# A linear-attention and MLP kernel: the first five tiles written out piece by piece, in order of arrival

## The chip, the cores and the metric

One core of a Trainium2 chip. The metric is the device time of one execution in microseconds, as a median over runs; every comparison is made with runs of the kernel before on the same chip, in the fast state. Ratios are computed as the mean time of one kernel's fast runs over that of the other's of the same rounds, so they are not quite the ratio of the quoted medians. A profile's span is 1.7 to 1.9 us shorter than the timed execution it belongs to.

## The reference

```python
# r, k, v: (4, 8, 768, 48); per step t, with a (48 x 48) state per head
cur = outer(u * k_t, v_t);  y_t = r_t @ (state + cur);  state = w[:, None] * state + outer(k_t, v_t)
# then on x = y as (4, 768, 384):
xn = (x - mean) / sqrt(var + 1e-6) * g_ln
out = x + relu(xn @ w_ch1) @ w_ch2          # w_ch1: 384 x 1536, w_ch2: 1536 x 384
```

## The kernel before

The sequence is cut into chunks of 128 steps, 24 "tiles" in all. A tile goes through: load r, k, v; scale r (GpSimd) and k (VectorE) by powers of w; transposes on TensorE and a copy on ScalarE (`trs`); scores on TensorE, a mask on VectorE (`A`), the state (`Z`); values (`y`), x, statistics; centering on ScalarE (`xn`), the pow for the deviation on GpSimd (`rs`); transposes (`xT`); "ups" (x by w1, ReLU on ScalarE) and "downs" (by w2), then `ot` and the store. Ups of two tiles run together as a group (`GT = 2`, 256 columns). All five engines run their instructions in the order in which the program lists them. `fill(n)` puts in up to n queued ups or downs, which keeps TensorE busy while attention waits for other engines.

```python
scale(0); transposes(0)
for s in range(NT):
    if s + 1 < NT: scale(s + 1)            # r on GpSimd, k on VectorE, one tile ahead
    scores(s)
    if s >= 1: center(s - 1)               # xn on ScalarE, rs on GpSimd (last of a pair)
    if s == 1: scale_w1(0)
    if s + 4 < NT: load(s + 4)
    if s == 1: nc.gpsimd.dma_start(out=w2_sb[:], in_=w2_src)
    fill(2)
    if s + 1 < NT: transposes(s + 1)       # before the values of this tile
    fill(2)
    if s >= 1: ln_transposes(s - 1)        # queues the ups of a finished pair
    values(s)
    if s == 1: scale_w1(1); scale_w1(2)
    fill(2)
# ... (cut: end of the program)
```

Loads before the loop: w_c, chunk 0 (k on ScalarE's queue), chunk 1, w1, chunk 2, chunk 3.

## Time and profile before

| | before |
|---|---|
| time, median | 174.94 us of 3 runs (175.16 of 4 with the run beside the change) |
| span of the profile | 173.4 us |
| TensorE busy | 146.9 us, 85% |
| VectorE, ScalarE, GpSimd busy | 66%, 55%, 43% |
| first down matmul, last matmul ends | 39.3, 169.8 us |

The page's busy slices and the timelines are in the prediction. Two more views are wanted later. First, busy time by stretch of 10 us: for each engine (TensorE, its weight loads, VectorE, ScalarE, GpSimd) the busy time and the number of instructions, then the granted clock (the share of TensorE's full clock that the trace records), the DMA share and GB/s.

```profile
20.00:30.00 10.00, 4.04 (x44) 2.81 (x43) 7.84 (x16) 5.02 (x8) 9.08 (x12) 1.00 1.33 179
30.00:40.00 10.00, 10.00 (x113) 7.84 (x113) 5.65 (x13) 5.90 (x12) 2.66 (x5) 1.00 1.13 194
40.00:50.00 10.00, 9.24 (x107) 6.91 (x106) 8.19 (x17) 6.09 (x11) 5.54 (x8) 1.00 0.76 143
```

TensorE is 40% busy from 20 to 30 us and nearly full from there on. Second, of the groups by line, the two large matmul groups; the columns behind the last bar are TensorE's idle time just before them and what ended it.

```profile
L374 PE MATMUL hp<-xT,w_sb 128*128 128x256 bf16 x432 | 58.0, 276 | 2.7 <-ACT xT L359 2.7
L396 PE MATMUL o<-w_sb,hT 128*128 128x384 bf16 x288 | 56.3, 326 | 0.9 <-DVE ot L405 0.8
```

In the steady state, nearly all that is left of TensorE's idle time is ups that wait for ScalarE's xT and one down that waits for the output tile.

### The profile page before, as it was taken

To read this page: it belongs to the slowest core of one execution; us is meant where nothing else is said; L and a number is where in the kernel's file an instruction comes from. 1 tells how busy PE (TensorE), PEld (TensorE's weight loads), DVE (VectorE), ACT (ScalarE), POOL (GpSimd) and SP (SyncE) were. 2 spreads that over 40 slices of the span, in tenths; PEclk is the share of its full clock that TensorE was granted. 3 is DMA by queue.
4 is the path that set the end of the run, shared out by engine and by line. 5 is a ranking of instruction groups with operands and counts; after the bars stand their busy time and mean duration, and the time that the engine had idled before them with its cause. 6 is when DMAs were issued, how large, how long until landed. Compare 5 with 4: busy or idle time off the path is not lost.

```text
span 173.4 us, 4126 instructions
## 1 busy us (share of the span) xinstructions
PE 146.9 (85%) x1646; PEld 110.4 (64%) x1646; DVE 113.9 (66%) x236; ACT 94.6 (55%) x173; POOL 74.7 (43%) x119
## 2 busy tenths in 40 slices
PE   0327453998999999999999999999999999999981
PEld 0215242695786877777768767777778687686640
DVE  4407959549788688678767976786768667840111
ACT  0313273385585774675666647656666577565410
POOL 2292699057426553374255335642752453120000
PEclk9999999999999999999999999999999999999999
DMA  5999999999954755874686568546954011101121
GB/s 98 163 351 316 186 181 177 200 190 150 199 114 95 169 114 104 167 155 89 140 165 147 110 110 183 131 105 135 181 112 119 0 49 45 33 18 45 45 93 46
DMA packets 82739, 22.69 MB, mean 131 GB/s; under 512 B 76960, under 2 KB 81568, under 8 KB 82720
## 3 DMA queue, kind: packets, MB, share of 16 engines
q1 hardware_dynamic: 78896, 21.04, 59.1%
q0 software_dynamic: 1552, 1.18, 4.6%
q10 hardware_dynamic: 2272, 0.20, 1.1%
q8 instruction: 13, 0.21, 0.6%
q14 instruction: 6, 0.05, 0.1%
HBM read 18.88 MB, written 4.72 MB: 136 GB/s over the span
## 4 chain that ended last, share of the span: by engine, by line
PE 76%; DVE 10%; ACT 8%; issue 2%; DMA 1%; POOL 1%; DVEq 0%; ACTq 0%
PE hp L374 27%; PE o L396 25%; PE tr L214 7%; PE at L229 4%; ACT xT L359 3%; ACT trs L216 3%; PE tr L358 3%; PE s L240 2%; PE s L260 2%; PE y L312 2%; DMA w_c<-in_w_dram 1%; PE s L251 1%; PE y L300 1%; DVE ot L405 1%; DVE stats L326 1%
## 5 line engine op out<-in xcount | busy, mean ns | idle before, releaser
L374 PE MATMUL hp<-xT,w_sb 128*128 128x256 bf16 x432 | 58.0, 276 | 2.7 <-ACT xT L359 2.7
L396 PE MATMUL o<-w_sb,hT 128*128 128x384 bf16 x288 | 56.3, 326 | 0.9 <-DVE ot L405 0.8
L381 ACT ACTIVATE hT<-hp 128x512 bf16<-128x512 f32 x72 | 42.9, 598 | 22.6 <-PE hp L374 22.1
L279 POOL TENSOR_TENSOR Vb<-vf,cc 128x384 f32<-128x384 f32 x24 | 20.2, 841 | 66.2 <-ACT cc L277 66.2
L374 PEld LDWEIGHTS <-w_sb 128*128 128x128 bf16 x432 | 40.3, 99 | 9.0 <-issue 3.8
L396 PEld LDWEIGHTS <-hT 128*128 128x128 bf16 x288 | 27.6, 98 | 13.6 <-issue 1.4
L270 DVE TENSOR_TENSOR A<-at,mask 128x512 bf16<-128x512 f32 x48 | 30.7, 682 | 1.3 <-PE at L229 1.3
L216 ACT COPY trs<-tr 128x1024 bf16<-128x1024 bf16 x24 | 24.2, 1009 | 13.2 <-PE tr L214 13.2
L218 DVE TENSOR_TENSOR q<-trs 128x512 bf16<-128x512 bf16 x24 | 12.3, 512 | 25.2 <-ACT trs L216 25.1
L205 POOL TENSOR_TENSOR sc<-rk,F 128x384 bf16<-128x384 f32 x24 | 23.9, 997 | 2.4 <-DMA rk<-in_r_dram 2.4
L405 DVE SCALAR_TENSOR_TENSOR ot<-o,rs,x 128x384 f32<-128x384 f32 x24 | 14.6, 609 | 14.6 <-PE o L396 14.6
L214 PE MATMUL tr<-ident,sc 128*128 128x128 bf16 x192 | 16.7, 234 | 7.4 <-POOL sc L205 5.7
L214 PEld LDWEIGHTS <-sc 128*128 128x128 bf16 x192 | 13.6, 105 | 10.2 <-POOL sc L205 6.5
L322 DVE TENSOR_TENSOR x<-y,Vb 128x384 f32<-128x384 f32 x24 | 13.4, 556 | 9.1 <-PE y L312 9.0
L337 ACT ACTIVATE xn<-x,mv 128x384 bf16<-128x384 f32 x24 | 14.8, 617 | 0.7 <-DVE mv L330 0.7
L277 ACT COPY cc<-s 128x8 f32<-128x8 f32 x24 | 4.0, 166 | 20.2 <-PE s L260 17.8
L359 ACT COPY xT<-tr 128x384 bf16<-128x384 bf16 x24 | 11.5, 480 | 5.5 <-PE tr L358 5.5
L204 DVE TENSOR_TENSOR sc<-rk,F 128x384 bf16<-128x384 f32 x24 | 14.4, 599 | 0.0
L207 POOL CAST vv<-vf 128x384 bf16<-128x384 f32 x24 | 14.3, 595 | 0.0
L326 DVE BATCH_NORM_STATS2 stats<-x 128x6 f32<-128x384 f32 x24 | 13.5, 561 | 0.8
L358 PE MATMUL tr<-ident,xn 128*128 128x128 bf16 x72 | 8.2, 225 | 4.3 <-ACT trs L216 4.3
L229 PE MATMUL at<-trs 48*128 48x128 bf16 x192 | 10.4, 233 | 1.7 <-ACT trs L216 1.7
(49 smaller groups left out, 119.1 us busy)
## 6 DMA issues: line engine op xcount, KB each, us to landing
rk<-in_r_dram SPq DMA_DIRECT2D x24, 192.0 KB, 4.1
vf<-in_v_dram SPq DMA_DIRECT2D x24, 192.0 KB, 4.2
out_dram<-ot SPq DMA_DIRECT2D x24, 192.0 KB, 2.0
rk<-in_k_dram SPq DMA_DIRECT2D x23, 192.0 KB, 3.4
w_f<-in_moe_w_ch_dram SPq DMA_DIRECT2D x3, 768.0 KB, 6.1
w_sb<-in_moe_w_ch_dram POOLq DMA_DIRECT2D x1, 1152.0 KB, 12.5
rk<-in_k_dram ACTq DMA_DIRECT2D x1, 192.0 KB, 3.6
w_p<-in_w_dram ACTq DMA_DIRECT2D x2, 0.8 KB, 4.3
```

Of the source, the lines that this page charges most:

```text
L205: nc.gpsimd.tensor_tensor(out=sc[:, 0, :, :D], in0=rk_t[i][:, 0], in1=F2[:, 0], op=ALU.mult)
L214: nc.tensor.transpose(out=tp[:, j, :], in_=sc[:, j, :], identity=ident[:])
L216: nc.scalar.copy(out=tr[:], in_=tp[:].rearrange("p (a q) t -> p a q t", a=2))
L229: nc.tensor.matmul(out=at[:, par, p, :], lhsT=tr[p0 : p0 + D, 1, p, :], rhs=tr[p0 : p0 + D, 0, p, :], start=True, stop=True,)
L270: nc.vector.tensor_tensor(out=A[:, par], in0=at[:, par], in1=mask[:].unsqueeze(1).to_broadcast([P, HP, P]), op=ALU.mult,)
L279: nc.gpsimd.tensor_tensor(out=Vb[:], in0=vf_t[i][:], in1=cc[:].unsqueeze(2).to_broadcast([P, H, D]), op=ALU.mult)
L326: nc.vector.bn_stats(out=stats[:], in_=x[:])
L359: nc.scalar.copy(out=xT_t[g][:, :, j * P : (j + 1) * P], in_=tp[:, :CK, :])
L374: nc.tensor.matmul(out=hp[:, f, :], lhsT=w1_sb[:, n, kc, fb * P : (fb + 1) * P], rhs=xT_t[g][:, kc, :], start=(kc == 0), stop=(kc == CK - 1),)
L381: nc.scalar.activation(out=hT_t[g][:, 2 * m : 2 * m + 2, :], in_=hp[:], func=ACT.Relu)
L396: nc.tensor.matmul(out=o[:, :C], lhsT=hT_t[g][:, fk, j * P : (j + 1) * P], rhs=w2_sb[:, fk, :], start=(fk == 0), stop=(fk == FK - 1),)
L405: nc.vector.scalar_tensor_tensor(out=ot[:], in0=o[:, :C], scalar=rs_t[g][:, j : j + 1], in1=x_t[i][:], op0=ALU.mult, op1=ALU.add,)
```

## The change

It wants to fill the lead-in. Chunks 0 to 2 are loaded before w1, and each tile's work is listed when its data should have arrived. The first four tiles are groups of one, so that ups can start with the first tile. w2 is issued behind tile 3's casts. The steady state changes too: ups two slots after their transposes, output tiles that alternate between `o` and the `hp` buffers, scales two tiles ahead.

```diff
-    load(0, nc.scalar) ... load(1); w1; load(2); load(3)
+    for i in range(3): load(i)
+    w1
+    for i in range(3, 5): load(i)
...
-                ups.append((clock[0] + 1, g, m))
+                ups.append((clock[0] + 2, g, m))
+    group_len = [1] * 4 + [GT] * ((NT - 4) // GT)
...
-            o_t[i] = ps.tile([P, 512], FP32, name="o")
+            alt = not ups and i % 2
+            o_t[i] = ps_h.tile([P, 512], FP32, name="hp") if alt else ps.tile([P, 512], FP32, name="o")
...
+    scores(2)
+    center(1)
+    scale_w1(1)
+    fill(1)
+    ln_transposes(1)
+    values(2)
+    scale_w1(2)
+    fill(1)
+    center(2)
+    drain_ups()
+    for s in (3, 4):
+        scale_r(s)
+        scale_k(s)
+        transposes(s)
+        if s == 3:
+            nc.gpsimd.dma_start(out=w2_sb[:], in_=w2_src)
+        load(s + 2)
+        ln_transposes(s - 1)
+        scores(s)
+        drain_ups()
+        values(s)
+        center(s)
+    ln_transposes(4)
+    drain_ups()
+    w2_ready[0] = True
+    scale_r(5)
+    scale_k(5)
+    fill(6)
+    transposes(5)
+    scale_r(6)
+    load(7)
+    fill(3)
+    for s in range(5, NT):
+        ...  (the loop of before, scales two tiles ahead)
```

(Cut: the F factors in two PSUM tiles, tile 0's copy split between ScalarE and VectorE, w1's scaling without VectorE, seven hT buffers, a down that may follow a down when no up can run, tiles 0 to 2 up to scores(2).)

More of the change, by code (lines that the diff above doesn't have):

```diff
@@ L64, with load @@
     rk_t, vf_t, v_t = {}, {}, {}
-    def load(i, k_eng=None):
+    def load(i):
         b, c = divmod(i, NCH)
@@ L70, in load @@
         vf = ld.tile([P, H, D], FP32, name="vf")
-        (k_eng or nc.sync).dma_start(out=rk[:, 1], in_=k[b, :, s0 : s0 + L, :].rearrange("h t d -> t h d"))
-        nc.sync.dma_start(out=rk[:, 0], in_=r[b, :, s0 : s0 + L, :].rearrange("h t d -> t h d"))
-        nc.sync.dma_start(out=vf[:], in_=v[b, :, s0 : s0 + L, :].rearrange("h t d -> t h d"))
+        for dst, src in ((rk[:, 0], r), (rk[:, 1], k), (vf[:], v)):
+            nc.sync.dma_start(out=dst, in_=src[b, :, s0 : s0 + L, :].rearrange("h t d -> t h d"))
         rk_t[i], vf_t[i] = rk, vf
@@ L77 @@
     nc.sync.dma_start(out=w_c[:], in_=bass.AP(tensor=w.tensor, offset=w.offset, ap=[[1, P], [P, CK]]))
-    load(0, nc.scalar)
     w_p = const.tile([P, HP], FP32, name="w_p")
@@ L90 @@
     nc.scalar.dma_start(out=g_sb[:], in_=moe_g_ln.rearrange("(kc p) -> p kc", p=P))
-    load(1)
     NW = 3
@@ L95 @@
     w1_src = moe_w_ch1.rearrange("(kc p) (n f) -> p n kc f", p=P, n=NW)
-    for n in range(NW):
-        nc.sync.dma_start(out=w1_f[:, n], in_=w1_src[:, n])
     w1_sb = const.tile([P, NW, CK, FW], BF16, name="w1_sb")
@@ L100 @@
     w2_src = moe_w_ch2.rearrange("(fk p) c -> p fk c", p=P)
-    load(2)
-    load(3)
+    for i in range(3):
+        load(i)
+    for n in range(NW):
+        nc.sync.dma_start(out=w1_f[:, n], in_=w1_src[:, n])
+    for i in range(3, 5):
+        load(i)
     ident_f = const.tile([P, P], FP32, name="ident_f")
@@ L146 @@
         n *= 2
-    fps = ps.tile([P, 2, 512], FP32, name="at")
-    F2 = const.tile([P, 2, H, D], FP32, name="F2")
-    for a in (0, 1):
+    Fr = const.tile([P, H, D], FP32, name="Fr")
+    Fk = const.tile([P, H, D], FP32, name="Fk")
+    for dst, src in ((Fr, T[:, 0:CK, 0:L]), (Fk, T[:, CK : 2 * CK, 1 : L + 1])):
+        fps = ps_h.tile([P, 512], FP32, name="hp")
         for kc in range(CK):
-            src = T[:, CK + kc, 1 : L + 1] if a else T[:, kc, 0:L]
-            nc.tensor.transpose(out=fps[:, a, kc * P : (kc + 1) * P], in_=src, identity=ident_f[:])
-    nc.scalar.copy(out=F2[:, 0], in_=fps[:, 0, :C].rearrange("p (h d) -> p h d", h=H))
-    nc.vector.tensor_copy(out=F2[:, 1], in_=fps[:, 1, :C].rearrange("p (h d) -> p h d", h=H))
+            nc.tensor.transpose(out=fps[:, kc * P : (kc + 1) * P], in_=src[:, kc], identity=ident_f[:])
+        cp = nc.scalar.copy if dst is Fr else nc.vector.tensor_copy
+        cp(out=dst[:], in_=fps[:, :C].rearrange("p (h d) -> p h d", h=H))
+    g_neg = const.tile([P, CK], FP32, name="g_neg")
+    nc.vector.tensor_scalar(out=g_neg[:], in0=g_sb[:], scalar1=-1.0, scalar2=None, op0=ALU.mult)
     wl = const.tile([P, HP], FP32, name="wl")
@@ L174 @@
         )
-    g_neg = const.tile([P, CK], FP32, name="g_neg")
     def scale_w1(n):
-        if n == 0:
-            nc.vector.tensor_scalar(
-                out=g_neg[:], in0=g_sb[:], scalar1=-1.0, scalar2=None, op0=ALU.mult
-            )
-        nc.scalar.activation(
-            out=w1_sb[:, n, 0], in_=w1_f[:, n, 0], func=ACT.Copy, scale=g_neg[:, 0:1]
-        )
-        nc.vector.tensor_scalar(
-            out=w1_sb[:, n, 1], in0=w1_f[:, n, 1], scalar1=g_neg[:, 1:2], scalar2=None, op0=ALU.mult
-        )
+        for kc in range(2):
+            nc.scalar.activation(
+                out=w1_sb[:, n, kc], in_=w1_f[:, n, kc], func=ACT.Copy, scale=g_neg[:, kc : kc + 1]
+            )
         nc.gpsimd.tensor_scalar(
@@ L200, with scale_k, scale_r @@
     tr_t, cc_t, Z_t, A_t, x_t, mv_t, xn_t, q_t, st = {}, {}, {}, {}, {}, {}, {}, {}, {}
-    def scale(i):
-        sc = sc_bufs[i % NSC]
-        nc.vector.tensor_tensor(out=sc[:, 1, :, :D], in0=rk_t[i][:, 1], in1=F2[:, 1], op=ALU.mult)
-        nc.gpsimd.tensor_tensor(out=sc[:, 0, :, :D], in0=rk_t[i][:, 0], in1=F2[:, 0], op=ALU.mult)
+    def scale_k(i):
+        nc.vector.tensor_tensor(
+            out=sc_bufs[i % NSC][:, 1, :, :D], in0=rk_t[i][:, 1], in1=Fk[:], op=ALU.mult
+        )
+    def scale_r(i):
+        nc.gpsimd.tensor_tensor(
+            out=sc_bufs[i % NSC][:, 0, :, :D], in0=rk_t[i][:, 0], in1=Fr[:], op=ALU.mult
+        )
         vv = ld.tile([P, H, D], BF16, name="vv")
@@ L215, in transposes @@
         tr = sb3.tile([P, 2, HP, P], BF16, name="trs")
-        nc.scalar.copy(out=tr[:], in_=tp[:].rearrange("p (a q) t -> p a q t", a=2))
+        if i == 0:
+            nc.scalar.copy(out=tr[:, 0], in_=tp[:, :HP])
+            nc.vector.tensor_copy(out=tr[:, 1], in_=tp[:, HP:])
+        else:
+            nc.scalar.copy(out=tr[:], in_=tp[:].rearrange("p (a q) t -> p a q t", a=2))
         q = sb2.tile([P, HP, P], BF16, name="q")
@@ L326, in values @@
         nc.vector.bn_stats(out=stats[:], in_=x[:])
-        g, j = divmod(i, GT)
+        g, j = tile_group[i]
         if j == 0:
@@ L333, in center @@
     def center(i):
-        g, j = divmod(i, GT)
+        g, j = tile_group[i]
+        n = group_len[g]
         mv = mv_t[g]
@@ L340, in center @@
         xn_t[i] = xn
-        if j == GT - 1:
+        if j == n - 1:
             rs = sm.tile([P, GT], FP32, name="rs", bufs=8)
             nc.gpsimd.tensor_scalar(
-                out=rs[:], in0=mv[:, :, 1], scalar1=1e-6, scalar2=1.0, op0=ALU.add, op1=ALU.mult
+                out=rs[:, :n], in0=mv[:, :n, 1], scalar1=1e-6, scalar2=1.0, op0=ALU.add, op1=ALU.mult
             )
-            nc.gpsimd.tensor_tensor(out=rs[:], in0=rs[:], in1=expo[:], op=ALU.pow)
+            nc.gpsimd.tensor_tensor(out=rs[:, :n], in0=rs[:, :n], in1=expo[:, :n], op=ALU.pow)
             rs_t[g] = rs
     xT_t, hT_t, o_t, rs_t = {}, {}, {}, {}
+    group_len = [1] * 4 + [GT] * ((NT - 4) // GT)
+    assert sum(group_len) == NT
+    tile_group = [(g, j) for g, n in enumerate(group_len) for j in range(n)]
+    group_first = [sum(group_len[:g]) for g in range(len(group_len))]
+    FB = FW // P
+    NM = 3
+    PM = FK // NM
     def ln_transposes(i):
-        g, j = divmod(i, GT)
+        g, j = tile_group[i]
         if j == 0:
@@ L359, in ln_transposes @@
         nc.scalar.copy(out=xT_t[g][:, :, j * P : (j + 1) * P], in_=tp[:, :CK, :])
-        if j == GT - 1:
-            for m in range(NU):
-                ups.append((clock[0] + 1, g, m))
-    NU = FK // 2
-    FB = FW // P
+        if j == group_len[g] - 1:
+            for m in range(FK * group_len[g] * P // 512):
+                ups.append((clock[0] + 2, g, m))
     def up(g, m):
+        gw = group_len[g] * P
+        nf = 512 // gw
         if m == 0:
-            hT_t[g] = sb3.tile([P, FK, GW], BF16, name="hT", bufs=5)
-        hp = ps_h.tile([P, 2, GW], FP32, name="hp")
-        for f in range(2):
-            n, fb = divmod(2 * m + f, FB)
+            hT_t[g] = sb3.tile([P, FK, GW], BF16, name="hT", bufs=7)
+        hp = ps_h.tile([P, 512], FP32, name="hp")
+        for f in range(nf):
+            n, fb = divmod(nf * m + f, FB)
             for kc in range(CK):
                 nc.tensor.matmul(
-                    out=hp[:, f, :],
+                    out=hp[:, f * gw : (f + 1) * gw],
                     lhsT=w1_sb[:, n, kc, fb * P : (fb + 1) * P],
-                    rhs=xT_t[g][:, kc, :],
+                    rhs=xT_t[g][:, kc, :gw],
                     start=(kc == 0),
@@ L380, in up @@
                 )
-        nc.scalar.activation(out=hT_t[g][:, 2 * m : 2 * m + 2, :], in_=hp[:], func=ACT.Relu)
-        if m == NU - 1:
-            for j in range(GT):
+        nc.scalar.activation(
+            out=hT_t[g][:, nf * m : nf * (m + 1), :gw],
+            in_=hp[:].rearrange("p (f t) -> p f t", f=nf),
+            func=ACT.Relu,
+        )
+        if nf * (m + 1) == FK:
+            for j in range(group_len[g]):
                 for d in range(NM):
-                    downs.append((clock[0] + 1, g * GT + j, d))
-    NM = 3
-    PM = FK // NM
+                    downs.append((clock[0] + 1, group_first[g] + j, d))
     def down(i, m):
-        g, j = divmod(i, GT)
+        g, j = tile_group[i]
         if m == 0:
-            o_t[i] = ps.tile([P, 512], FP32, name="o")
+            alt = not ups and i % 2
+            o_t[i] = ps_h.tile([P, 512], FP32, name="hp") if alt else ps.tile([P, 512], FP32, name="o")
         o = o_t[i]
@@ L421 @@
     last_o = [-9]
-    down_from = [99]
+    w2_ready = [False]
     ups, downs = [], []
@@ L429, in fill @@
             can_up = ups and ups[0][0] <= clock[0]
-            can_down = downs and downs[0][0] <= clock[0] and clock[0] >= down_from[0]
-            if can_down and downs[0][2] == 0 and last_o[0] >= clock[0]:
+            can_down = downs and downs[0][0] <= clock[0] and w2_ready[0]
+            if can_down and can_up and downs[0][2] == 0 and last_o[0] >= clock[0]:
                 can_down = False
@@ L444, in fill, with drain_ups @@
                 break
-    W2_SLOT = 1
-    DOWN_SLOT = 4
-    scale(0)
-    transposes(0)
-    for s in range(NT):
-        if s == DOWN_SLOT:
-            down_from[0] = clock[0]
-        if s + 1 < NT:
-            scale(s + 1)
-        scores(s)
-        if s >= 1:
-            center(s - 1)
-        if s == 1:
-            scale_w1(0)
-        if s + 4 < NT:
-            load(s + 4)
-        if s == W2_SLOT:
-            nc.gpsimd.dma_start(out=w2_sb[:], in_=w2_src)
+    def drain_ups():
+        clock[0] += 2
+        while ups:
+            _, g, m = ups.pop(0)
+            up(g, m)
+    scale_k(0)
+    scale_r(0)
+    transposes(0)
+    scale_r(1)
+    scores(0)
+    scale_k(1)
+    transposes(1)
+    values(0)
+    scale_r(2)
+    scores(1)
+    center(0)
+    scale_w1(0)
+    scale_k(2)
+    transposes(2)
+    ln_transposes(0)
+    values(1)
+    clock[0] += 1
+    fill(1)
[6 more added lines that the diff above has]
+    scale_w1(2)
+    fill(1)
+    center(2)
[8 more added lines that the diff above has]
+        ln_transposes(s - 1)
+        scores(s)
+        drain_ups()
[13 more added lines that the diff above has]
+        scores(s)
+        if s > 5:
+            center(s - 1)
+        if s + 2 < NT and s > 5:
+            scale_r(s + 2)
+        if s == 5:
+            scale_k(6)
+            scale_r(7)
+        if s + 3 < NT:
+            load(s + 3)
         fill(2)
@@ L467 @@
         fill(2)
-        if s >= 1:
+        if s > 5:
             ln_transposes(s - 1)
         values(s)
-        if s == 1:
-            scale_w1(1)
-            scale_w1(2)
+        if s + 2 < NT:
+            scale_k(s + 2)
         fill(2)
```

## The prediction

> **What bounds the kernel now.** I read the page's busy slices first, then the matmul timeline of the first 40 us, the chain that ended last, the groups by line, and GpSimd's timeline.
>
> ```profile
> PE   0327453998999999999999999999999999999981
> POOL 2292699057426553374255335642752453120000
> PEclk9999999999999999999999999999999999999999
> DMA  5999999999954755874686568546954011101121
> ```
>
> A slice is 4.3 us. TensorE is at 90% or more from slice 7 (about 30 us) to the end, and badly used before that. So the time is a lead-in, then TensorE work at its own pace, then a tail. The pace comes from two marks in the chain, the same step six pairs of tiles apart:
>
> ```profile
> 65.60 0.49 ACT xT L359
> ...
> 135.97 0.49 ACT xT L359
> ```
>
> 70.37 us for 12 tiles is 5.86 us a tile, 24 tiles are 140.7 us, and the span is 173.4: 33 us are lead-in and tail. Of a tile's 5.86, the up matmuls take 18 x 109 ns = 1.96 (12 in 1.31 us in the chain), the down matmuls 12 x 163 ns = 1.96 (4 in 0.65 us), and the attention part the other 1.94.
>
> How much is done when the steady state starts? The matmul timeline:
>
> ```profile
> 31.03 2.72 PE L374 MATMUL hp<-xT,w_sb 128*128 128x256 bf16 x12
> ...
> 34.83 1.47 PE L374 MATMUL hp<-xT,w_sb 128*128 128x256 bf16 x12
> 36.14 0.61 PE L214 MATMUL tr<-ident,sc 128*128 128x128 bf16 x8
> 36.59 1.47 PE L374 MATMUL hp<-xT,w_sb 128*128 128x256 bf16 x12
> 37.90 0.33 PE L358 MATMUL tr<-ident,xn 128*128 128x128 bf16 x3
> ```
>
> At 37.9 us four tiles of attention (7.8 us), one early transpose (0.45) and one pair's ups (3.93) are done: 12.1 us of work. The deficit (clock less work done) is 25.8 us, and that is what the change attacks. From 37.9 the rest, 128.6 us, would end at 166.5; the last matmul really ends at 169.8, so 3.3 us leak later, and 3.6 follow for the last output.
>
> **What the Trainium skill says.** (1) "TensorE: Matmul & The Clock Gate", Part 1: the array runs at half rate until about 3.4 us of sustained activity. The trace agrees by pace: 12 equal matmuls take 2.72 us at 31.03 and 1.47 at 34.83, though the granted clock reads 9 throughout. So everything before 34.8 us ran at half pace. (2) The same page, "Back-to-back issue gap", gives about 81 ns for a 128-column matmul with its own weight load. The trace differs and decides: eight transposes, each with its own weights, take 0.45 us in the chain, 56 ns each. (3) "DMA: Bandwidth & Descriptors", Specifications: below 512 B a transfer misses line rate. It agrees: chunks 2 and 3, in 192-byte rows, land 1.05 us apart for 192 KB (187 GB/s); in w1's time slices show about 405 GB/s. (4) "PSUM — Partial Sum Buffer", Terms: two engines must not access one bank at once, two reads included. In the trace the two copies of the F factors out of one PSUM tile run one after the other (7.41 and 7.92, VectorE having waited for ScalarE).
>
> **The change part by part.** *Loads.* w1 steps back behind chunk 2. From the recorded landings (v1 9.99, r2 18.13, v2 19.18, w1's last third 15.94, v3 22.33, v4 25.50) I estimate v2 at 13, w1 at 15, 17 and 19, v3 and v4 unchanged. Chunk 2 is 6 us earlier, w1 3 us later. k0 returning to the sync queue costs one 0.5 us issue.
>
> *F factors.* In two PSUM tiles the copies overlap: 0.5 us. This gains little, because GpSimd's scale of r0 starts only at 10.39, after its w_p and WLZ work, which begins at 6.92 when w_p lands. With k0 off the ScalarE queue w_p may land 0.6 us earlier: r0 at 9.8. Splitting tile 0's copy between ScalarE and VectorE gains nothing if reads of a bank are serialized.
>
> *Groups of one.* A tile's ups become 36 x 56 ns = 2.0 us against 1.96, and 3 ReLUs of 0.60 as before. Almost free at full pace; at half pace 12 take 1.3 us. But each of these tiles now does the rs pair on GpSimd, in the middle of this stage:
>
> ```profile
> 26.64 0.82 POOL L279 TENSOR_TENSOR Vb<-vf,cc 128x384 f32<-128x384 f32 x1
> 27.55 0.25 POOL L343 TENSOR_SCALAR rs<-mv 128x2 f32<-128x2 f32 x1
> 27.88 0.93 POOL L346 TENSOR_TENSOR rs<-rs,expo 128x2 f32<-128x2 f32 x1
> 28.79 0.99 POOL L205 TENSOR_TENSOR sc<-rk,F 128x384 bf16<-128x384 f32 x1
> ```
>
> The scale of r can only follow rs, as engines take their instructions in program order. Before, a tile's scale stands ahead of the previous tile's scores. In the new code scale_r(3) stands behind rs(2), and scale_r(4) behind rs(3), which need the finished statistics of the previous tile. That is a serial loop through all engines.
>
> ```profile
> L270 DVE TENSOR_TENSOR A<-at,mask 128x512 bf16<-128x512 f32 x48 | 30.7, 682 | 1.3 <-PE at L229 1.3
> L216 ACT COPY trs<-tr 128x1024 bf16<-128x1024 bf16 x24 | 24.2, 1009 | 13.2 <-PE tr L214 13.2
> L322 DVE TENSOR_TENSOR x<-y,Vb 128x384 f32<-128x384 f32 x24 | 13.4, 556 | 9.1 <-PE y L312 9.0
> L326 DVE BATCH_NORM_STATS2 stats<-x 128x6 f32<-128x384 f32 x24 | 13.5, 561 | 0.8
> ```
>
> *The lead-in walked through*, each step by these durations, in program order (all estimates). Tile 0: r0 scaled at 10.8, transposes 11.9, copies 13, scores and mask 15, Z and the scale of k1 (now behind Z) 16. Tile 1: transposes 17, copy 18, q and tile 0's x and statistics 19.8, mask and Z 21.6, k2 22.1. Tile 2: transposes 23.2, copy 24.2, tile 0's layer-norm transposes and copy 25.3; up(0,0), cold, 26.9; scores(2) 28.3; cc and Vb 29.4; rs(1) 30.6; GpSimd's part of w1's second third 31.5. Only then can up(0,1) run, and TensorE stands behind it: 33. ReLU and tile 1's xT 34.1, ScalarE's two pieces of w1's last third (0.72 each) 35.5, up(0,2) 37, tile 1's three ups, partly cold, 40.
>
> Then tile 3: transposes 0.5, copy 1.0, layer-norm transposes and scores 1.0, tile 2's ups 2.0, values 0.4, x, stats and mv 1.4: 46.3. rs 1.2, scale_r(4) 1.0: 48.5. Tile 4 the same way with tile 3's ups: 6.3, so 54.8; xn 0.6 and the last layer-norm transposes 0.2: 55.6. TensorE has about 4 us of work in each of these 8 us turns. Only then come the downs. w2, issued by GpSimd behind tile 3's casts at about 38, took 12.5 us to land before and does so by about 50: not the bound.
>
> *The sum.* At 55.6 the new kernel has done five tiles of attention (9.7) and four of ups (8.0): 17.7, a deficit of 37.9 against 25.8, so 12 us worse. Another 1.5 may go to half pace after the idle gaps. On the other side, ups wait two slots instead of one (TensorE's idle time before them is 2.7 us in all) and alternate output tiles stay in the hp buffers at the end (the 0.63 us waits for ot between down groups, three of them, 1.9): at most 4, I count 3.5. Net +10: 174.9 + 10 = 185; I take 184.5.
>
> **Rivals.** (a) The intent: data in arrival order and early ups fill the lead-in. For it: chunk 2 comes 6 us sooner and the first ups at about 25 instead of 31 us. Were the serial loop to cost half of my figure, the lead-in would end near 48 with the same work, a deficit of 30, less 3.5 saved: about equal; with TensorE at full pace throughout, 170. Against it: DMA is saturated to 25 us either way, and my walk finds tile 3 waiting for engines, not for data. (b) w2 becomes the bound: issued 15 us later than before (22.38) and beside chunks 5 and 6. If it landed at 60, another 4 us: 189. Against it: those loads would be finished by 32. (c) Loads now lead by one slot less; a load stuck behind an output on the sync queue could starve a slot of the steady state. At 0.3 us for each of 18 slots that is 190. Against it: loads land in about 4 us and a slot is 5.86.
>
> **Range and chances.** The walk has some 40 steps with borrowed durations; 15% of the 45 us from 10 to 55 is 7 us. So 178 to 191. To be faster by 2% (under 171.4) the walk would have to be wrong by 13 us, for which a false order on GpSimd would be needed: 9%. Within 2% (to 178.4): 10%. Slower: 81%.
>
> **What would show it.** The first up matmuls near 25 us and the second group only near 31, idle behind w1's scaling. GpSimd's r scale of tile 3 near 37 and of tile 4 near 47, directly behind rs. The first down matmuls near 55 with w2 long landed. Half-full slices from 20 to 55 us; then 5.7 to 5.86 us a tile; no wait for ot at the end. Wrong if scale_r(4) starts before 42 or downs before 48.

## The result, and the profile after

190.26 us (median of 4 runs, of which one was slow, 192.96) against 175.16: the ratio is 1.0857, with a 95% interval from 1.0807 to 1.0908. The change is 8.6% slower. The profiled run has a span of 188.7 us against 173.4.

The page's slices of the changed kernel, 4.7 us each (TensorE, GpSimd, granted clock, DMA):

```profile
PE   0445466971959967999999999999999999999992
...
POOL 2863434515430158265253743537445264311000
PEclk9999996699586998799999999999999999999999
DMA  5999996292000599913938749197591951020112
```

TensorE is full from slice 16 (75 us) instead of slice 7 (30 us), with holes at slices 9 (42 us), 11 (52 us) and 14 to 15 (66 to 75 us). DMA is idle in slices 10 to 12 (47 to 61 us): data is not the bound there. The granted clock falls to half several times between slices 6 and 16, which it never did before once it was up.

The timeline of TensorE through the turn of tile 4 (its pass through all the engines, from the scales to the statistics) and into the first downs:

```profile
39.46 2.35 PE L383 MATMUL hp<-xT,w_sb 128*128 128x128 bf16 x36
41.64 0.33 PE L302 MATMUL y<-Z,trs 128*128 128x96 bf16 x4
41.81 0.36 PE L314 MATMUL y<-vv,A 128*128 128x48 bf16 x8
45.81 0.62 PE L212 MATMUL tr<-ident,sc 128*128 128x128 bf16 x8 [3.63 <-POOL sc L201]
...
49.21 4.04 PE L383 MATMUL hp<-xT,w_sb 128*128 128x128 bf16 x36
...
56.02 0.34 PE L368 MATMUL tr<-ident,xn 128*128 128x128 bf16 x3 [2.24 <-ACT xn L340]
56.20 3.36 PE L408 MATMUL o<-w_sb,hT 128*128 128x384 bf16 x12
```

After tile 3's values (y, ended 42.2) TensorE has nothing for 3.63 us until GpSimd has scaled r. The same 36 ups take 2.35 us for tile 2 and 4.04 for tile 3. The first downs start at 56.2 us, against 39.3 before. GpSimd in that gap:

```profile
43.75 0.40 POOL L346 TENSOR_SCALAR rs<-mv 128x1 f32<-128x1 f32 x1 [2.96 <-DVE mv L332]
44.23 0.56 POOL L349 TENSOR_TENSOR rs<-rs,expo 128x1 f32<-128x1 f32 x1
44.77 0.98 POOL L201 TENSOR_TENSOR sc<-rk,Fr 128x384 bf16<-128x384 f32 x1
```

It waits 2.96 us for tile 3's statistics, does rs, and only then scales r of tile 4, whose r had landed at 23.35.

Busy time by stretch, with the columns as before:

```profile
40.00:50.00 10.00, 5.25 (x78) 4.34 (x76) 4.46 (x10) 4.06 (x7) 3.41 (x6) 0.83 0.45 70
50.00:60.00 10.00, 7.76 (x61) 5.71 (x59) 2.49 (x6) 2.89 (x5) 3.37 (x5) 0.67 0.01 2
60.00:70.00 10.00, 8.88 (x95) 5.67 (x93) 5.31 (x11) 2.36 (x4) 3.07 (x4) 0.98 0.72 162
70.00:80.00 10.00, 7.97 (x89) 6.68 (x90) 8.05 (x17) 6.68 (x12) 5.54 (x8) 0.83 1.07 197
```

From 40 to 60 us no engine is over half busy but TensorE, and that one runs partly at half clock: a chain through all engines, one at a time. From 60 to 80 TensorE is short of work a second time, in the handover to the loop:

```profile
68.96 0.39 PE L212 MATMUL tr<-ident,sc 128*128 128x128 bf16 x4
70.93 0.40 PE L212 MATMUL tr<-ident,sc 128*128 128x128 bf16 x4 [1.58 <-DVE sc L196]
72.43 0.33 PE L368 MATMUL tr<-ident,xn 128*128 128x128 bf16 x3 [1.10 <-ACT trs L218]
```

To say how much each stretch costs, I worked out a **deficit** from each trace: the clock less the work that TensorE has started by then. Each matmul counts with its full-clock slot (start to start in the steady state of before: up 109 ns at 256 columns and 55.5 at 128, down 163, transposes 55.5, and so on for the small ones; the six transposes of the setup are not counted). The deficit rises only where TensorE idles or runs slowly; all kernels have the same 133.4 to 133.6 us of such work. The column "end" is taken at the last matmul's start.

```
at us               30    40    50    60    70    80   120   160   end
before            25.3  27.5  29.0  29.7  30.2  30.8  32.7  34.9  36.1
after             24.1  29.3  35.7  41.1  43.2  47.2  48.4  49.8  51.2
a_scale_early     24.4  29.8  34.3  38.6  42.6  44.4  45.8  47.0  48.4
a_overlap         24.4  28.9  32.6  33.7  38.6  38.9  40.2  41.5  42.9
a_spread          24.4  29.0  35.7  40.9  43.0  44.0  45.3  46.6  47.9
a_overlap_spread  24.4  28.9  32.6  34.1  35.9  36.0  37.3  39.0  40.0
a_six_ones        24.4  30.0  36.1  42.4  43.3  46.8  50.9  52.3  53.7
b_serial          24.3  29.6  35.5  36.1  36.8  37.2  39.4  41.5  43.1
b_loads           24.9  26.4  27.6  28.3  28.8  29.3  31.2  33.7  34.6
b_ones            23.9  27.4  28.0  30.1  31.3  31.8  33.7  35.9  37.1
b_steady          25.2  27.2  27.5  27.5  27.8  28.0  28.7  30.5  30.4
b_ones_steady     23.3  25.0  25.7  25.9  26.0  26.2  26.8  28.6  28.5
```

The 15.1 us at the end come about like this. At 30 us the changed kernel is 1.2 us ahead. From 30 to 60 us it loses 12.6 against before (17.0 less 4.4). Of these, 3.0 (5.2 less 2.2) are lost by 40 us, while the last ups of tile 0 and those of tile 1 wait for w1's scaling and run at half clock (29.6 to 36.4 us); the other 9.6, from 40 to 60 us, are the turns of tiles 3 and 4. From 60 to 80 it loses another 5.0 (6.1 less 1.1): the handover. From 80 us on it wins 1.3 (4.0 against 5.3).

### The profile page after: what moved, and what is told of

It reads as the page before. It is cut to its first block, busy times and chain, and to the rows that moved or that the text cites. A ratio compares the mean times of both kernels' runs of the same rounds, so it can differ in the third digit from the quotient of the medians.

```text
span 188.7 us, 4275 instructions
## 1 busy us (share of the span) xinstructions
PE 154.5 (82%) x1718; PEld 116.7 (62%) x1718; DVE 110.7 (59%) x234; ACT 96.5 (51%) x176; POOL 76.3 (40%) x123
## 4 chain that ended last, share of the span: by engine, by line
PE 70%; DVE 12%; ACT 7%; POOL 4%; issue 3%; DMA 2%; ACTq 0%; DVEq 0%; POOLq 0%
PE hp L383 28%; PE o L408 13%; PE hp L408 7%; PE tr L212 6%; ACT trs L218 5%; PE at L231 4%; DVE ot L417 2%; PE tr L368 2%; DVE sc L196 2%; DVE stats L328 2%; DVE x L324 2%; PE y L314 2%; PE s L242 2%; PE s L262 2%; DVE A L272 2%
## 5 line engine op out<-in xcount | busy, mean ns | idle before, releaser
L383 PE MATMUL hp<-xT,w_sb 128*128 128x256 bf16 (+1 forms) x504 | 60.6, 277 | 4.1 <-ACT w_sb L180 3.0
L383 PEld LDWEIGHTS <-w_sb 128*128 128x128 bf16 x504 | 47.0, 108 | 10.5 <-ACT w_sb L180 3.6
L390 ACT ACTIVATE hT<-hp 128x512 bf16<-128x512 f32 x72 | 42.4, 601 | 17.4 <-PE hp L383 15.6
L218 ACT COPY trs<-tr 128x1024 bf16<-128x1024 bf16 x23 | 23.2, 1010 | 22.2 <-PE tr L212 22.2
L220 DVE TENSOR_TENSOR q<-trs 128x512 bf16<-128x512 bf16 x24 | 11.7, 487 | 33.8 <-ACT trs L218 33.8
L408 PE MATMUL o<-w_sb,hT 128*128 128x384 bf16 x156 | 30.5, 336 | 0.7 <-DVE ot L417 0.7
L408 PE MATMUL hp<-w_sb,hT 128*128 128x384 bf16 x132 | 25.2, 330 | 0.0
L201 POOL TENSOR_TENSOR sc<-rk,Fr 128x384 bf16<-128x384 f32 x24 | 24.2, 1009 | 0.5 <-PE tr L212 0.5
L324 DVE TENSOR_TENSOR x<-y,Vb 128x384 f32<-128x384 f32 x24 | 13.3, 552 | 15.1 <-PE y L314 15.0
L417 DVE SCALAR_TENSOR_TENSOR ot<-o,rs,x 128x384 f32<-128x384 f32 x13 | 7.9, 610 | 14.1 <-PE o L408 14.1
L196 DVE TENSOR_TENSOR sc<-rk,Fk 128x384 bf16<-128x384 f32 x24 | 13.9, 580 | 0.0
```

Source lines behind the costliest of these rows:

```text
L196: nc.vector.tensor_tensor(out=sc_bufs[i % NSC][:, 1, :, :D], in0=rk_t[i][:, 1], in1=Fk[:], op=ALU.mult)
L201: nc.gpsimd.tensor_tensor(out=sc_bufs[i % NSC][:, 0, :, :D], in0=rk_t[i][:, 0], in1=Fr[:], op=ALU.mult)
L218: nc.scalar.copy(out=tr[:], in_=tp[:].rearrange("p (a q) t -> p a q t", a=2))
L324: nc.vector.tensor_tensor(out=x[:], in0=y[:, :C], in1=cc_t[i][:].rearrange("p h d -> p (h d)"), op=ALU.add)
L383: nc.tensor.matmul(out=hp[:, f * gw : (f + 1) * gw], lhsT=w1_sb[:, n, kc, fb * P : (fb + 1) * P], rhs=xT_t[g][:, kc, :gw], start=(kc == 0) ...
L390: nc.scalar.activation(out=hT_t[g][:, nf * m : nf * (m + 1), :gw], in_=hp[:].rearrange("p (f t) -> p f t", f=nf), func=ACT.Relu,)
```

## The experiments

Twelve kernels ran; all gave correct results. "a_" starts from the changed kernel, "b_" from the kernel before. My theory: the order of the instruction streams makes the turns of tiles 3 and 4 serial (scale_r(i+1) behind the statistics and rs of tile i). The rivals: the load order, and the groups of one.

### a_scale_early: only the scales moved

```diff
     ln_transposes(1)
+    scale_k(3)
     values(2)
     scale_w1(2)
+    scale_r(3)
...
-        scale_r(s)
-        scale_k(s)
         transposes(s)
...
         drain_ups()
+        if s == 3: scale_r(4); scale_k(4)
         values(s)
```

> The changed kernel with one thing moved: the scales of r and k of tiles 3 and 4 stand ahead of the statistics of tiles 2 and 3 in GpSimd's and VectorE's program (nothing else). My theory (the lead-in is long because scale_r(i+1) is behind rs(i), a serial loop through all engines): tile 4's transposes start near 42.3 us instead of 45.8, the first down matmuls near 52 instead of 56.0, the total is 186 to 187 (3.5 us less than 190.3). Rival 1 (the load order is to blame: w1 behind chunk 2, w2 behind chunk 4): no change, 190 within 1. Rival 2 (the groups of one are to blame, 128-column matmuls at half clock): no change, 190 within 1.

Measured: 187.82 us, ratio to before 1.0756 (the change: 1.0857). The first downs start at 53.4 us instead of 56.2. So moving four calls, with data, groups and loads untouched, brings back 1.0% (the medians differ by 2.4 us), where I had expected 3.5 us; both rivals said nothing would move. Tile 4's transposes start at 42.50 us instead of 45.81. But the hole is not gone, it has moved: after them TensorE idles for 2.69 us until ScalarE's copy (trs), which stands behind tile 3's centering and so behind the same statistics. GpSimd's scale is only the first link of the chain.

### a_overlap: the two turns overlapped

```diff
-    for s in (3, 4): scale_r(s) ... center(s)      # as in the change
+    scale_r(3); fill(1); center(2); transposes(3); <w2>; load(5)
+    scale_r(4); scale_k(4); drain_ups()
+    ln_transposes(2); scores(3); transposes(4); load(6); drain_ups()
+    values(3); center(3); scores(4); ln_transposes(3)
+    values(4); center(4); drain_ups()
```

(scale_k(3) stands before values(2), as above.)

> The changed kernel with the turns of tiles 3 and 4 overlapped: scales early, transposes(3) ahead of tile 1's ups, transposes(4) ahead of tile 2's ups and of values(3), tile 3's ups behind values(4), w2 issued as before behind tile 3's casts. Load order and groups of one stay. My theory: about 8 us of the turns' latency hide behind ups; first down matmuls near 48 us, total 182 to 183. Both rivals: no change, 190 within 1.5. If the total falls by much less than the first downs come forward, the gain is lost again at the handover (filler used up).

Measured: 181.75 us, ratio 1.0405, just under the expected 182 to 183. TensorE's timeline at the first downs:

```profile
49.13 2.11 PE L408 MATMUL o<-w_sb,hT 128*128 128x384 bf16 x12
```

They come 7.1 us earlier and at full clock (2.11 us for the 12 instead of 3.36). At 60 us the deficit is 33.7 instead of 41.1. The two turns' order is thus worth half of the loss, and the same groups of one and loads run beside it. The halved clock after 46.7 and 56.9 us is gone together with the idle time, so the half counts both. The deficit still rises by 4.9 from 60 to 70 us: the handover is untouched.

### b_loads: the load order alone

```diff
     load(1)
+    load(2)
     <w1>
-    load(2)
     load(3)
```

> The kernel before with only the load order of the change: chunks 0 to 2, then w1, then chunk 3. My theory: the load order costs nothing, since before waited for chunk 2 (2.4 us at 18.2) and w1 is scaled only at 21.4 us; 172 to 176. Rival 1: w1 coming 3 us later holds up the ups and it is slower, 180 or more. Rival 2: says nothing, 175.

Measured: 174.10 us, ratio 0.9972 (0.9925 to 1.0018): the same time. The first rival is out, for the order of w1 and chunk 2; w2's late issue by itself was not run, but in the changed kernel w2 landed at 45.0 us and the first downs, at 56.2, waited for xn.

### b_ones: the groups of one alone

```diff
-    (pairs)
+    group_len = [1] * 4 + [GT] * ((NT - 4) // GT)
-    hT bufs=5
+    hT bufs=7
```

> The kernel before with only the first four tiles as groups of one (and 7 hT buffers as in the change). My theory: nearly free, as 36 matmuls of 128 columns cost 2.0 us against 1.96 at full clock, and ups can start one tile earlier; 172 to 177. Rival 2: half-clock small matmuls and the additional rs on GpSimd cost a good part of the 15 us; 180 or more. Rival 1: 175.

Measured: 176.56 us, ratio 1.0136 (1.0057 to 1.0215). They cost 1.4% (unclear by the 2% rule), not the 8.6. The deficit shows that they do what they were meant to do by 30 us (23.9 against 25.3) and lose it again later, 1.4 us of it between 50 and 60 us (2.1 against 0.7 before), where downs wait for ot.

### b_serial: the suspected cause put into the kernel before

```diff
-        if s + 1 < NT:
+        if s + 1 < NT and s not in (2, 3):
             scale(s + 1)            # the same for transposes(s + 1), and for center in slots 3 and 4
...
         fill(2)
+        if s in (2, 3):
+            center(s)
+            scale(s + 1)
+            transposes(s + 1)
```

> The kernel before with the suspected cause put in: in slots 2 and 3 the scales and transposes of the next tile stand behind the scores, values, statistics and centering of this tile, as in the change's turns; load order, pairs and steady state as before. Theory: each of the two turns exposes the chain x, statistics, scale, transposes, copy (some 4 us, of which one or two ups hide 1.3): 5 to 8 us more, 180 to 183. Rival (the order only matters because of groups of one or the load order): 175 to 176.

Measured: 183.17 us, ratio 1.0469, just above the expected 180 to 183. TensorE's timeline has the changed kernel's hole:

```profile
37.10 0.36 PE L312 MATMUL y<-vv,A 128*128 128x48 bf16 x8
41.62 1.04 PE L214 MATMUL tr<-ident,sc 128*128 128x128 bf16 x8 [4.16 <-POOL sc L205]
```

After the hole the transposes run at half clock (1.04 us instead of 0.61). The order alone makes the good kernel 4.7% slower.

### a_six_ones and a_spread: what the handover lacks

```diff
-    group_len = [1] * 4 + [GT] * ((NT - 4) // GT)
+    group_len = [1] * 6 + [GT] * ((NT - 6) // GT)      # a_six_ones
```

> The changed kernel with six groups of one instead of four: tile 4's ups can run right after its layer-norm transposes (near 56 us) and give three more down groups, so TensorE has filler between 62 and 73 us, where the changed kernel ran out of downs before the pair of tiles 4 and 5 had ups. Theory (the handover costs 3.1 us of idle and some 1.7 us at half clock): TensorE's idle time in the 30 us after the first down falls from 3.1 to about 1 us, total 186 to 188 (2.5 to 4 less than 190.3). Rival (groups of one are what costs): 2 more of them make it slower, 191 or more. Rival (handover idle costs nothing): 190 within 1.

Measured: 192.70 us, ratio 1.1028: a miss, slower by 1.6% than the change. It is the number that the rival (groups of one are what costs) gave; b_ones speaks against that rival, where four of them cost 1.4%. Two rows of TensorE's timeline show the first reason:

```profile
57.93 3.80 PE L383 MATMUL hp<-xT,w_sb 128*128 128x128 bf16 x36 [0.62 <-ACT xT L369]
61.53 2.15 PE L408 MATMUL o<-w_sb,hT 128*128 128x384 bf16 x12
```

Tile 4's ups ran at once, at half clock, and put off everything else (the downs begin at 61.5). The hole itself only moved: the deficit rises by 0.9 from 60 to 70, but by 7.6 from 70 to 120, against 5.2 for the change. More filler was not the remedy. Nine of the twelve queued downs are run before scores(5), so I left the amount alone and changed only when it is used:

```diff
-    fill(6)
+    fill(2)
     transposes(5)
...
     load(7)
-    fill(3)
+    fill(2)                                            # a_spread
```

> The changed kernel with only the number of fillers in the handover changed: 2 and 2 instead of 6 and 3 ahead of scores(5), so that downs are left for slots 5 and 6. Theory (the downs are used up in one go, and then TensorE waits for the attention chain of tiles 6 and 7 between 66 and 74 us): the clock less the work done, which rises by 6.1 us from 60 to 80 us in the changed kernel, rises by 3 us less, total near 187. If what holds slots 5 and 6 up is not the filler but the waits for the late loads of chunks 7 and 8 or the order on VectorE: 190 within 1.

Measured: 187.12 us, ratio 1.0692. The deficit's rise from 60 to 80 us falls from 6.1 to 3.1, as expected. So the timing of the filler matters. How it does is shown only in part: after 60 us TensorE's idle stretches fall from 3.0 us (0.31, 1.58, 1.10) to 2.1 (1.04, 1.10), and the halved clock from 74.0 to 77.4 us is gone, worth up to 1.7 us (an estimate: half of 3.4). My reading is that while TensorE ran downs in a block, attention did not advance, and then attention had nothing beside it. What is left waits for VectorE's scale of k and ScalarE's copy, so the order on VectorE, the rival, may still hold a part. With the turns overlapped as well (a_overlap_spread):

> The overlapped turns of a_overlap and the spread fillers together. Theory: 181.75 less the 3 us of the handover, 178.5 to 179.5. If the fillers don't matter: 181.5 within 1.

Measured: 179.24 us, ratio 1.0251. The gains add up: of the 8.6% this takes away 6.1. At 50 us the deficit is 3.6 above that of before, and that remains to the end (40.0 against 36.1). I did not take it apart further; TensorE there waits for w1's scaling and tile 4's centering, in an order I left as it was.

### a_warm: what the half clock costs

```diff
         values(s)
+        keep_warm(40 if s == 3 else 25)     # matmuls of 128 columns that nobody reads
         center(s)
```

> The changed kernel with matmuls that nobody reads (40 of 128 columns behind values(3), 25 behind values(4), into an output tile not yet in use), in time in which TensorE was idle. Theory (the idle gaps of the serial turns also drop TensorE to half clock from 46.7 to 53.5 and 56.9 to 60.3 us): the clock stays at full there, tile 3's ups take 2.2 us instead of 4.0, the first downs start near 53.5 instead of 56.0, total about 187 (3 us less). Rival (the half clock is hidden behind the latency of the other engines): 190 within 1.

Measured: 187.84 us (median of all four), ratio 1.0728; its profile fell in a run that was slow (191.48) while the other three were fast (186.41 to 187.96), so only the total is compared. By the ratios it is 1.2% below the change, some 2 us: part of the idle time's cost is the half clock after it. How much of it lies in which turn stays open. In the slow run's trace the clock was halved all the same from 47.8 to 54.7 us.

### b_steady, b_loads_steady, b_ones_steady: the steady-state parts

```diff
-                ups.append((clock[0] + 1, g, m))
+                ups.append((clock[0] + 2, g, m))
-            o_t[i] = ps.tile([P, 512], FP32, name="o")
+            alt = not ups and i % 2
+            o_t[i] = ps_h.tile([P, 512], FP32, name="hp") if alt else ps.tile([P, 512], FP32, name="o")
-            if can_down and downs[0][2] == 0 and last_o[0] >= clock[0]:
+            if can_down and can_up and downs[0][2] == 0 and last_o[0] >= clock[0]:
-    hT bufs=5
+    hT bufs=7
```

> The kernel before with only the steady-state parts of the change: output tiles alternate with the hp buffers when no ups are queued, a down may follow a down when no up can run, ups two slots later, seven hT buffers. Theory (the change's steady state is 0.1 us a tile faster and has fewer waits at the end: 11.52 us a pair against 11.73): 2 to 3.5 us less, 171.5 to 173. If the changed kernel's pace comes from something else (scales two tiles ahead), 174.5 within 1.

Measured: 169.37 us, ratio 0.9703: 3.0% faster than before, more than expected. The groups by line answer to the two shown of before (the second row has the downs into `o`; the other 132 write `hp`, with no idle time before them):

```profile
L381 PE MATMUL hp<-xT,w_sb 128*128 128x256 bf16 x432 | 54.3, 276 | 0.1
...
L405 PE MATMUL o<-w_sb,hT 128*128 128x384 bf16 x156 | 29.6, 326 | 0.7 <-DVE ot L414 0.7
```

The 2.7 us of ups waiting for xT are down to 0.1, while the idle time before downs hardly changes (a single wait for ot of 0.7 us, near the end). Altogether TensorE idles 0.8 us after its first down instead of 4.2. That is 3.4 of the 5.7 us; the rest is time that counts as busy while matmuls start later than their slots, which the deficit sees: from 40 us to the end it rises by 3.2 instead of 8.6. How it divides between the four edits was not run.

> The kernel before with the new load order and the steady-state parts together, without the written-out lead-in and without groups of one. Theory: the two gains add up, 0.5 and 2 to 3.5 us: 171 to 172.5, faster than both kernels. If they don't add, 172.5 to 174.

Measured: 169.59 us, ratio 0.9709. That is under both expected ranges, because the steady-state parts alone gave more (0.9703). The two don't add: beside them the new load order is worth nothing, as it was alone within the noise (0.9972).

> The kernel before with the steady-state parts and the first four tiles as groups of one. Groups of one alone were 1 us ahead at 30 us and 1 us behind at the end, where waits for ot cost them; with alternating outputs that part should vanish: 168.5 to 170, equal to the steady parts alone within 1%.

Measured: 167.59 us, ratio 0.9574 (0.9538 to 0.9611), a little better than expected. It beats both kernels. With alternating outputs the groups of one keep their early lead (deficit 25.0 at 40 us, against 27.2 for b_steady).

This kernel has the groups and the steady-state parts of the change but the old order of the lead-in and the old loads, and it is the fairer measure of what the rest of the change costs: 22.7 us of deficit (51.2 less 28.5). Of those a_overlap_spread brings back 11.2. The other 11.5 are not explained by any run here; w1's scaling without VectorE, the scales two tiles ahead and the split F factors were never run alone.

## Why the prediction was right

**Lead-in, right.** The step "scale_r(3) stands behind rs(2), and scale_r(4) behind rs(3)", a serial loop through all engines, is what the trace shows (3.63 us of TensorE's idle time ended by GpSimd's scale), what removing it gives back (a_overlap, 4.5% of 8.6) and what putting it in costs (b_serial, 4.7%). The loop goes on through ScalarE: with GpSimd's scale moved alone, only 1.0% came back. The walk set the end of the lead-in at 55.6 us; the first downs started at 56.2.

**Inside the walk two errors cancelled, by luck.** It was late at first: w_p landed at 3.62 and 4.26 us, where I had put it 0.6 us ahead of 6.92, so r0 was scaled at 7.94 instead of 9.8; rs on one column takes 0.76 us for tile 0 (0.19 and 0.57) and 1.02 in the turn of tile 3 (43.75 to 44.77), not 1.2; tile 3's scale of r came at 33.05 instead of near 37. It was then too quick: from tile 3's transposes (36.67) to the end of the lead-in took 19.3 us where the walk has 15.6, mostly because tile 4's turn ran at half clock: in it tile 3's ups took 4.04 us for 2.0. For half clock I had charged 1.5 us in all, beside "partly cold" ups of tile 1.

**Loads and w2, right.** Chunk 2 was complete at 13.38, w1's thirds at 15.23, 17.10 and 19.06, v3 and v4 at 22.30 and 25.45; the estimates were 13, then 15, 17 and 19, and unchanged. w2 landed at 45.0, before the 50 I gave it. Rival (b), w2, did not happen. For rival (c), late loads, GpSimd waited 0.8 us for v in the handover, and no more.

**Groups of one, right in the main.** Almost free: 1.4% alone, and a gain together with alternating outputs.

**The copy split over two engines gains nothing, right, but not shown for the reason given.** ScalarE and VectorE read the same PSUM bank one after the other, in the changed kernel, and need 1.03 us together where one copy takes 1.01:

```profile
10.12 0.59 ACT L215 COPY trs<-tr 128x512 bf16<-128x512 bf16 x1 [2.78 <-PE tr L212]
10.73 0.42 DVE L216 COPY trs<-tr 128x512 bf16<-128x512 bf16 x1 [1.32 <-ACT trs L215]
```

VectorE's copy waits there for a semaphore that ScalarE's copy raises, so it is the program that puts them in turn; what the chip would do without it doesn't show. The same holds for the two F copies of before that the prediction's point (4) reads as a sign of it: they lie in two banks of one tile (each copy's half is 512 FP32 values a partition, and "PSUM — Partial Sum Buffer", Terms, gives a bank 2 KiB a partition), VectorE waited for ScalarE's semaphore (7.41 and 7.92), and so they say nothing of two reads of one bank. In two tiles VectorE waited for its transposes alone (7.50).

**The sum, off by 5 us.** Net 10 was predicted and 15.1 measured (190.26 less 175.16), near the upper end of the range. The sum was 12 and 1.5 for the lead-in, less 3.5. Measured by the deficit, the lead-in cost 11.4 by 60 us, the handover 5.0, and the steady state gave back 1.3. So the term that is missing is the handover, which the working did not have at all: it took TensorE to be busy as soon as downs could run. The 6.1 us by which the deficit rose there are 3.1 in a_spread, so half of it goes with the block of nine downs. The term that is mis-sized is "at most 4, I count 3.5", the steady-state gain. In the kernel before the same parts gain 5.7 us (175.03 less 169.37), 2.9 of deficit from 80 us on; why only 1.3 came through in the changed kernel was not run.

Two readings under that term were wrong. The pace of 5.86 us a tile was taken as pure work, with "the attention part the other 1.94" as the remainder. By the slots of the deficit a tile has 5.56 us of work (133.4 over 24), so some 0.3 us a tile of waiting was counted as work, and the "3.3 us" that leak later were too few: the deficit of before rises by 8.6 from 40 us to the end. And the three "0.63 us waits for ot" are steps of VectorE on the chain; TensorE was idle before only one down (0.8 us in the group row above), and the changed kernel still has such a wait (0.71 us at 174.92), where the prediction wanted none.

**The intent was half right.** At 30 us the change is ahead by 1.2 us, with ups from 23.2 us on instead of 31.0; rival (a) had that part. The groups of one alone do as much, though (b_ones: 1.4 us ahead, ups from 24.3 us), with the old order and loads. The lead was lost when the two following turns were written one after the other.

## What to carry to other kernels

When engines run in program order, a lead-in written out by hand must keep the look-ahead of the loop it replaces: the first instruction of the next tile belongs ahead of the last wait of this one on every engine. Spread queued filler over the slots that have waits; a block of it delays the chain that it should cover. Test the parts of a large change one by one: here the steady-state and grouping parts were worth 4.3% and the rest hid it.

## What the Trainium skill lacked or had wrong

- "TensorE: Matmul & The Clock Gate", Part 1, and the trace's clock: the granted clock reads 1.00 from the start, yet 12 equal matmuls took 2.72 us at 31.03 and 1.47 at 34.83. The clock has no record before its first event (at 34.7 us in the kernel before), so the column says nothing about the cold start. No page says this.
- The same page, "Back-to-back issue gap": about 81 ns for a 128-column matmul in a stream with weight loads. Here eight such transposes take 0.45 us in the chain, 56 ns each, and the change's 36 ups of tile 2 take 2.35 us, 65 ns each with waits and the last one's end.
- The same page, on idle gaps of about 3.4 us: it fits the 3.63 us gap, after which the change's ups took 4.04 instead of 2.35 us. But the other three falls of the clock followed shorter idle stretches: at most 1.44 us before 29.6, 2.24 before 56.9, 1.58 and 1.10 before 74.0. Further down the page does tell of a clock that swings with frequent short idle stretches; how short they may be it does not say.
